# Gated attention and a top-1 expert layer on one core: score columns per query group, mirrors from the last two groups, and a first tile table during attention

## The chip, the cores and the metric

The kernel runs on one core of one Trainium2 chip. Its time is the device time of one execution in microseconds (us). Lower is better.

The engines named here are PE (TensorE: matmuls and transposes, writing to PSUM), ACT (ScalarE), DVE (VectorE), POOL (GpSimd, which here issues DMAs and scatters) and SP (SyncE, which here issues DMAs and DMA transposes).

## The reference

```python
scores = (1.0 / S) * np.matmul(z, z.transpose(0, 2, 1))   # z: 8 x 2816 x 64
attn = np.maximum(scores, 0.0) ** 2
x = (u * np.matmul(attn, v)).reshape(N, D)                # N = 22528, D = 256
y_dense = np.maximum(x @ w1_dense, 0.0) @ w2_dense         # F = 512
logits = x @ w_gate                                        # 8 experts
e = np.argmax(logits, axis=1)                              # one expert per token
gate = softmax(logits)[e]
out = y_dense + gate * (np.maximum(x @ w1[e], 0.0) @ w2[e])
```

The softmax line shortens the original; the rest is its arithmetic. For each batch the score matrix is symmetric: 22 x 22 blocks of 128 x 128.

## The kernel before

**Attention.** A row is 128 queries of a batch, so there are 22 rows per batch and 176 in all (the loop variable g). z is held twice side by side in zT, so that a score matmul contracts over 128 rows, and the scale is halved. `score_chunk` (lines 168 to 176) computes up to four neighbouring blocks of the upper triangle of the scores on PE, applies the relu on ACT into a float32 tile r, and squares r on DVE into the bfloat16 strip A. The blocks below the diagonal are not computed: `mirror` (lines 178 to 190) transposes blocks of A on PE and copies them to a tile T, two copies of three on ACT and one on DVE. `av` (line 223) adds up the 22 matmuls of a row, with A or T as weights and v as the moving operand, and issues the score chunks and mirrors of later rows between them, spread evenly, some seven rows ahead. `gate_x` (line 244) multiplies by u on DVE into `pay`, and SP transposes the row for the logits, which PE computes three rows later. After each 11 rows (a routing group, 16 in all) `route_a` and `route_b` find the expert, the gate and the position of each token, and `scatter` (line 313) writes the rows to the DRAM buffer `xs`, sorted by expert, with one indirect DMA per row on POOL.

**The table.** After the last routing, DVE works out which 256 rows of `xs` and which expert belong to each of 95 tiles (lines 402 to 466). A tile is 256 tokens of one expert.

**Experts.** For each tile SP fetches the tokens transposed (`fetch`, line 475), DVE copies the expert's weights (`expert`, line 487), PE runs `up` and `down` for the dense and for the expert weights, 32 matmuls of 256 columns, and `finish` (line 512) scales, adds and scatters the rows to the output.

**What sets the order.** PE, ACT, DVE and SP run their instructions in the order of the program. Only POOL's order is left to the framework, which may put a DMA there ahead of others. The queues run freely against one another, tied by semaphores. In PSUM the attention has three one-bank buffers for scores, two for transposes, two for the output of `av` and one for the logits; the expert stage opens pools of its own.

Of the kernel before, what the change touches and what calls it, by code (L numbers as in the profile page):

```python
# [15 lines left out]
P = 128  # L16
# [3 lines left out]
def kernel(  # L20
# [18 lines left out]
    assert D == 256 and dq == 64 and F == 512 and E == 8 and S % P == 0  # L39
# [3 lines left out]
    assert nK % G == 0  # L43
    T2 = 256
    NT = N // T2 + E - 1
    ROW = 288
    CAP = N
    XROWS = E * CAP

# [5 lines left out]
    const = ctx.enter_context(tc.tile_pool(name="const", bufs=1))  # L55


    WD = 2 * F + 4 * D
# [6 lines left out]
    ntri = const.tile([P, P], BF, name="ntri")  # L65
    smask = const.tile([P, E, G], F32, name="smask")
# [4 lines left out]
    pays = [const.tile([P, G, ROW], BF, name=f"pay{i}") for i in range(2)]  # L71

    zpool = ctx.enter_context(tc.tile_pool(name="zp", bufs=2))
# [17 lines left out]
    def load_v(b):  # L91
        vb = zpool.tile([P, nK, D], BF, name="vb")
        src = v[b].rearrange("(k p) d -> p k d", p=P)
        for h in range(2):
            k0, k1 = h * nK // 2, (h + 1) * nK // 2
            nc.gpsimd.dma_start(out=vb[:, k0:k1, :], in_=src[:, k0:k1, :])
        return vb

    zT_of, v_of = {}, {}
    make_identity(nc, ident[:])  # L100
    zn0 = load_z(0, parts=4)
    v_of[0] = load_v(0)
# [3 lines left out]
    nc.vector.memset(smask[:, :, 0], 0.0)  # L106
    for p_ in pays:
        nc.vector.memset(p_[:], 0.0)
    nc.vector.memset(ntri[:], -1.0)

# [5 lines left out]
    nc.vector.tensor_copy(desc8[:], ti[:])  # L116
# [3 lines left out]
    nc.vector.tensor_copy(ecap[:], te[:])  # L120
    nc.vector.tensor_copy(base[:], te[:])
    it = const.tile([P, NT], I32, name="it")
    sf = const.tile([P, NT], F32, name="sf")
    itf = const.tile([P, N // T2], F32, name="itf")
    nc.gpsimd.iota(it[:], pattern=[[1, NT]], base=0, channel_multiplier=0)
    nc.vector.tensor_copy(sf[:], it[:])
    nc.vector.tensor_scalar(out=itf[:], in0=sf[:, 0:N // T2], scalar1=float(T2), scalar2=None,
                            op0=ALU.mult)
    pj = const.tile([P, 2], I32, name="pj")
    pjf = const.tile([P, 2], F32, name="pjf")  # L130
    nc.gpsimd.iota(pj[:], pattern=[[P, 2]], base=0, channel_multiplier=1)
    nc.vector.tensor_copy(pjf[:], pj[:])
    one8 = const.tile([P, E], F32, name="one8")
    nc.vector.memset(one8[:], 1.0)

    nc.gpsimd.dma_start(out=wg[:], in_=moe_w_gate.rearrange("(c p) e -> p c e", p=P))


    with tc.tile_pool(name="aA", bufs=1) as aA, \
         tc.tile_pool(name="aT", bufs=2) as aT, \  # L140
         tc.tile_pool(name="aw", bufs=2) as aw, \
         tc.tile_pool(name="rt", bufs=2) as rt, \
         tc.tile_pool(name="psS", bufs=3, space=bass.MemoryType.PSUM) as psS, \
         tc.tile_pool(name="psV", bufs=2, space=bass.MemoryType.PSUM) as psV, \
         tc.tile_pool(name="psT", bufs=2, space=bass.MemoryType.PSUM) as psT, \
         tc.tile_pool(name="psL", bufs=1, space=bass.MemoryType.PSUM) as psL:


        zT_of[0] = zpool.tile([P, nK, P], BF, name="zT")
        for k0 in range(0, nK, 8):  # L150
            k1 = min(k0 + 8, nK)
            nc.vector.tensor_copy(zn0[:, k0:k1, 1, :], zn0[:, k0:k1, 0, :])
            zp = psT.tile([P, 8, P], BF, name="zp", tag="tp")
            for k in range(k0, k1):
                nc.tensor.transpose(out=zp[:, k - k0, :],
                                    in_=zn0[:, k, :, :].rearrange("p h d -> p (h d)"),
                                    identity=ident[:])
            nc.scalar.copy(zT_of[0][:, k0:k1, :], zp[:, :k1 - k0, :])

        A, T, mc = {}, {}, [0]  # L160

        def new_strip(b, k):
            n = nK - k
            A[b, k] = aA.tile([P, n, P], BF, name=f"A{k}", tag=f"A{k}",
                              bufs=2 if k < 4 else 1)

        def score_chunk(b, k, c0, c1):

            zT = zT_of[b]
            w = c1 - c0  # L170
            s_ps = psS.tile([P, 4, P], F32, name="s_ps")
            nc.tensor.matmul(out=s_ps[:, :w, :], lhsT=zT[:, k, :],  # L172
                             rhs=zT[:, k + c0:k + c1, :], start=True, stop=True)
            r = aw.tile([P, 4, P], F32, name="r", bufs=3)
            nc.scalar.activation(r[:, :w, :], s_ps[:, :w, :], AF.Relu, scale=0.5 / S)  # L175
            nc.vector.tensor_mul(A[b, k][:, c0:c1, :], r[:, :w, :], r[:, :w, :])  # L176

        def mirror(b, i, j0, j1):

            if j0 == 0:  # L180
                T[b, i] = aT.tile([P, nK - 1, P], BF, name="T")
            tp = psT.tile([P, 8, P], BF, name="tp", tag="tp")
            for j in range(j0, j1):
                nc.tensor.transpose(out=tp[:, j - j0, :], in_=A[b, i][:, 1 + j, :],  # L184
                                    identity=ident[:])
            mc[0] += 1
            if mc[0] % 3 == 0:
                nc.vector.tensor_copy(T[b, i][:, j0:j1, :], tp[:, :j1 - j0, :])  # L188
            else:
                nc.scalar.copy(T[b, i][:, j0:j1, :], tp[:, :j1 - j0, :])  # L190

        work = []
        total = 0
        strip_end = {}
        for b in range(B):
            for k in range(nK):
                n = nK - k
                nch = -(-n // 4)
                edges = [round(n * j / nch) for j in range(nch + 1)]
                for j in range(nch):  # L200
                    total += edges[j + 1] - edges[j]
                    work.append((total, b, k, edges[j], edges[j + 1], j == 0))
                strip_end[b, k] = total
        wi = [0]

        def chunks(upto):

            jobs = []
            while wi[0] < len(work):
                tot, b, k, c0, c1, first = work[wi[0]]  # L210
                if tot - (c1 - c0) >= upto:
                    break

                def job(b=b, k=k, c0=c0, c1=c1, first=first):
                    if first:
                        new_strip(b, k)
                    score_chunk(b, k, c0, c1)

                jobs.append(job)
                wi[0] += 1  # L220
            return jobs

        def av(b, i, jobs):

            o = psV.tile([P, D], F32, name="o")
            vb = v_of[b]
            done = 0
            for k in range(nK):
                lhsT = A[b, k][:, i - k, :] if k <= i else T[b, i][:, k - i - 1, :]
# [22 lines left out]
        def logits(g):  # L252
            q, j = divmod(g, G)
            if j == 0:
                lg_of[q] = psL.tile([P, G, E], F32, name="lg", tag="lg")
# [322 lines left out]
```

## Time and profile before

| | |
|---|---|
| median of 7 runs | 1053.87 us (1051.4 to 1054.25) |
| the profiled execution, its own time | 1051.9 us |
| its span | 1050.2 us |
| PE busy | 987.2 us (94%) |
| DVE busy | 733.8 us (70%) |
| ACT busy | 655.9 us (62%) |
| POOL busy | 520.9 us (50%) |
| mean clock granted to TensorE | 0.982 of full |

Matmuls are pipelined: the duration of one is longer than the distance to the next, so prices are read from distances. "Busy" of PE counts overlapping matmuls once. A wait line names the waiting engine, its tile and line, what released it, and then the total, the count and the longest. In the view by stage each engine has its busy time and, in brackets, its instructions; the granted clock, the mean busy share of the DMA engines (over 1 where transfers overlap) and GB/s follow. In the timeline the first number is the start, the second how long the merged run of instructions took.

### The profile page before, as it was taken

The numbers are of one execution on the slowest core, as the hardware profiler recorded it, in microseconds if no ns is written. First come the engines' busy times: TensorE is split into PE (matmuls) and PEld (weight loads), VectorE is DVE, ScalarE is ACT, GpSimd is POOL, SyncE is SP. The second block draws the span as 40 slices with busy tenths as digits, with TensorE's granted clock in tenths as the row PEclk, the third lists the DMA queues.
The fourth block names the chain that finished last, engine by engine and source line by source line (L and its number), as shares of the span: only waits on it lengthen the run. The fifth ranks groups of instructions, "written<-read, shape, count | busy, mean of one in ns | idle before, by whom it ended". The sixth has DMA issues, their size and how long they took to land. (4 is left out here: it accounts for less than half of the span.)

```text
span 1050.2 us, 25478 instructions
## 1 busy us (share of the span) xinstructions
PE 987.2 (94%) x9713; PEld 849.2 (81%) x9742; DVE 733.8 (70%) x1638; ACT 655.9 (62%) x994; POOL 520.9 (50%) x528
## 2 busy tenths in 40 slices
PE   5959999999999999999999999909999999999996
PEld 3848888888888888888888888808888888888885
DVE  5838778687787777787777786475666666666664
ACT  6836676776776776676677677205555555555553
POOL 7523452552642642633633524444666666666665
PEclk9989999999999999999999999959999999999999
DMA  8994844745656557367364323314545455555551
GB/s 144 177 166 74 144 107 69 137 104 82 125 97 102 104 103 118 90 111 116 91 114 107 77 68 84 79 36 97 119 110 105 109 120 100 121 107 121 110 113 44
DMA packets 223531, 110.37 MB, mean 105 GB/s; under 512 B 179630, under 2 KB 209070, under 8 KB 223408
## 3 DMA queue, kind: packets, MB, share of 16 engines
q0 software_dynamic: 75264, 79.47, 37.6%
q1 hardware_dynamic: 148144, 29.27, 17.2%
q8 instruction: 76, 1.25, 0.5%
q14 instruction: 47, 0.39, 0.1%
HBM read 61.54 MB, written 39.06 MB: 96 GB/s over the span
## 5 line engine op out<-in xcount | busy, mean ns | idle before, releaser
L176 DVE TENSOR_TENSOR A<-r 128x512 bf16<-128x512 f32 (+2 forms) x576 | 350.6, 624 | 138.9 <-ACT r L175 135.0
L175 ACT ACTIVATE r<-s_ps 128x512 f32<-128x512 f32 (+2 forms) x576 | 308.3, 548 | 129.6 <-PE s_ps L172 90.8
L230 PE MATMUL o<-vb,A 128*128 128x256 bf16 x2024 | 307.8, 273 | 11.3 <-DVE pay L247 10.9
L230 PE MATMUL o<-vb,T 128*128 128x256 bf16 x1848 | 304.0, 273 | 1.2
L501 ACT ACTIVATE h<-h_ps 128x1024 bf16<-128x1024 f32 x190 | 194.4, 1023 | 162.6 <-PE h_ps L498 156.8
L522 POOL DMA_INDIRECT out_dram<-ys,ix x190 | 204.9, 1078 | 137.7 <-DVE ys L520 90.4
L315 POOL DMA_INDIRECT xs<-pay,posi x176 | 196.0, 1114 | 105.4 <-issue 45.7
L230 PEld LDWEIGHTS <-A 128*128 128x128 bf16 x2024 | 180.5, 97 | 45.4 <-issue 11.3
L230 PEld LDWEIGHTS <-T 128*128 128x128 bf16 x1848 | 173.4, 98 | 40.2
L190 ACT COPY T<-tp 128x768 bf16<-128x768 bf16 (+4 forms) x208 | 166.8, 803 | 50.9 <-PE tp L184 47.3
L172 PE MATMUL s_ps<-zT 128*128 128x512 bf16 (+3 forms) x547 | 193.1, 354 | 1.1 <-ACT r L175 1.1
L241 POOL DMA_DIRECT2D ut<-in_u_dram x88 | 65.0, 741 | 226.7 <-DVE pay L247 112.2
L518 DVE TENSOR_SCALAR ys<-ye,me 128x256 f32<-128x256 f32 x190 | 83.2, 480 | 121.0 <-PE ye L508 121.0
L508 PEld LDWEIGHTS <-h 128*128 128x128 bf16 x1520 | 148.7, 98 | 17.9 <-ACT h L501 0.6
L184 PE MATMUL tp<-ident,A 128*128 128x128 bf16 x1848 | 154.5, 219 | 4.5 <-DVE T L188 2.8
L184 PEld LDWEIGHTS <-A 128*128 128x128 bf16 x1848 | 129.0, 98 | 14.6 <-issue 5.5
L498 PE MATMUL h_ps<-xT,w1d 128*128 128x256 bf16 x760 | 99.3, 274 | 22.7 <-DMA xT<-xs 22.7
L498 PEld LDWEIGHTS <-w1d 128*128 128x128 bf16 x760 | 74.6, 98 | 31.8 <-issue 22.9
L498 PE MATMUL h_ps<-xT,we 128*128 128x256 bf16 x760 | 99.3, 274 | 0.0
L508 PE MATMUL ye<-we,h 128*128 128x256 bf16 x760 | 98.5, 273 | 0.3 <-ACT h L501 0.3
L508 PE MATMUL yd<-w2d,h 128*128 128x256 bf16 x760 | 98.5, 273 | 0.0
L247 DVE TENSOR_TENSOR pay<-o,ut 128x256 bf16<-128x256 f32 x176 | 73.5, 418 | 25.2 <-DMA ut<-in_u_dram 15.1
(95 smaller groups left out, 570.3 us busy)
## 6 DMA issues: line engine op xcount, KB each, us to landing
ut<-in_u_dram POOLq DMA_DIRECT2D x88, 256.0 KB
vb<-in_v_dram POOLq DMA_DIRECT2D x16, 704.0 KB
wall<-in_moe_w_dram POOLq DMA_DIRECT2D x16, 256.0 KB
out_dram<-ys,ix POOLq DMA_INDIRECT x190
xT<-pay SPq DMA_TRANSPOSE x176
xs<-pay,posi POOLq DMA_INDIRECT x176
zn<-in_z_dram POOLq DMA_DIRECT2D x7, 352.0 KB
xT<-xs SPq DMA_TRANSPOSE x95
```

What stands on the lines that cost most here:

```text
L172: nc.tensor.matmul(out=s_ps[:, :w, :], lhsT=zT[:, k, :], rhs=zT[:, k + c0:k + c1, :], start=True, stop=True)
L175: nc.scalar.activation(r[:, :w, :], s_ps[:, :w, :], AF.Relu, scale=0.5 / S)
L176: nc.vector.tensor_mul(A[b, k][:, c0:c1, :], r[:, :w, :], r[:, :w, :])
L184: nc.tensor.transpose(out=tp[:, j - j0, :], in_=A[b, i][:, 1 + j, :], identity=ident[:])
L190: nc.scalar.copy(T[b, i][:, j0:j1, :], tp[:, :j1 - j0, :])
L230: nc.tensor.matmul(out=o[:], lhsT=lhsT, rhs=vb[:, k, :], start=(k == 0), stop=(k == nK - 1))
L315: ins = nc.gpsimd.indirect_dma_start(out=xs, out_offset=bass.IndirectOffsetOnAxis(ap=rs[q][:, j:j + 1], axis=0), in_=pays[q % 2][:, j, :]. ...
L498: nc.tensor.matmul(out=h_ps[:, f, :], lhsT=w1(c, f), rhs=xT[:, c, :], start=(c == 0), stop=(c == 1))
L501: nc.scalar.activation(h[:], h_ps[:], AF.Relu)
L508: nc.tensor.matmul(out=y[:, j, :], lhsT=h[:, f, j * P:(j + 1) * P], rhs=w2(f), start=(f == 0), stop=(f == 3))
L518: nc.vector.tensor_scalar(out=ys[:, j, :], in0=ye[:, j, :], scalar1=me[:, j, 0:1], scalar2=None, op0=ALU.mult)
L522: ins = nc.gpsimd.indirect_dma_start(out=out, out_offset=bass.IndirectOffsetOnAxis(ap=ix[:, j:j + 1], axis=0), in_=ys[:, j, :], in_offset= ...
```

## The change

Attention is reorganised by query groups: a batch's 22 rows are cut into groups of 2, 4, 4, 4, 4 and 4. A group has one tile A of 22 key blocks by up to 512 query columns (three such tiles in all). Its blocks are scores for all key blocks, above and below the diagonal, except those that belong to the two groups before it in the batch; these are mirrored from the earlier groups' tiles. A score step takes one or two pairs of key blocks, and a pair fills a two-bank PSUM tile, of which there are three; mirrors, logits and routing share these. The relu takes a pair at once. The square runs on DVE or on ACT, as a small model of the engines' clocks in the program decides while the program is written out; it also decides between which matmuls of `av` the steps go, up to two groups ahead. Mirrors go to DVE or ACT by the same model.

The loads of u go from POOL's queue to SP's. The logits of 11 rows are computed in one burst at their routing. The scatters are spread over more rows, each with a small DVE copy of its index, and a third `pay` tile is added. The expert stage shares the attention's PSUM tiles and the A tiles; `ye` and `yd` share two one-bank buffers, and ACT copies `yd` to SBUF, so that DVE joins scaling and adding in one instruction.

The tile table is made twice. From the first 14 routing groups, a table of 70 full tiles is worked out on DVE between rows 159 and 163, and the first fetches and weight copies are issued at rows 173 to 175. The other 25 tiles come from a second table, made during the expert stage. The two last routings' scatters are not waited for by the first 70 tiles.

The diff, cut to what the prediction speaks of:

```diff
+    Q1 = nQ - 2
+    NT1 = -(-(Q1 * G * P - E * (T2 - 1)) // T2)
+    NT2 = NT - NT1
...
+    NPAIR = 3
+    psS = pool("psS", NPAIR, space=bass.MemoryType.PSUM)
+    psY = pool("psY", 2, space=bass.MemoryType.PSUM)
...
     def load_u(g):
         ut = aw.tile([P, 2, D], F32, name="ut", bufs=3)
-            nc.gpsimd.dma_start(out=ut[:], in_=uf[:, g:g + 2, :])
+        nc.sync.dma_start(out=ut[:], in_=uf[:, g:g + 2, :])
...
+        for w in (2, 4, 4, 4, 4, 4):
+            groups.append((b, i, w))
...
+    clock = {"pe": 0.0, "act": 0.0, "dve": 0.0}
+    def spend(eng, t, after=0.0):
+        clock[eng] = max(clock[eng], after, clock["pe"]) + t
+        return clock[eng]
...
+    def scores(n, k):
...
+        s = psS.tile([P, 2, 4 * P], F32, name="s", tag="s")
+        for h in range(2):
+            nc.tensor.matmul(out=s[:, h, :c], lhsT=zT[:, k + h, :], rhs=zT[:, i0:i0 + w, :],
+                             start=True, stop=True)
+        clock["pe"] += 0.01 + c / 1200
+        r = aw.tile([P, 2, 4 * P], F32, name="r", bufs=3)
+        nc.scalar.activation(r[:, :, :c], s[:, :, :c], AF.Relu, scale=0.5 / S)
+        t = spend("act", 0.09 + c / 600, clock["pe"] + 0.2)
+        freed(t)
+        a = A[n][:, k:k + 2, :c]
+        if max(clock["dve"], t) + 0.07 + c / 480 > clock["act"] + 0.3 + c / 600:
+            nc.scalar.activation(a, r[:, :, :c], AF.Square)
+            t = spend("act", 0.05 + c / 600)
+        else:
+            nc.vector.tensor_mul(a, r[:, :, :c], r[:, :, :c])
+            t = spend("dve", 0.07 + c / 480, t)
...
+    def mirror(n, m, j, nj):
+        (b, i0, w), (_, j0, wj) = groups[n], groups[m]
+        tp = psS.tile([P, nj, w, P], BF, name="tp", tag="s")
...
+    def produce():
+        for n, (b, i0, w) in enumerate(groups):
+            src = [m for m in (n - 2, n - 1) if m >= 0 and groups[m][0] == b]
+            turned = {k for m in src for k in range(groups[m][1], groups[m][1] + groups[m][2])}
+            ks = [k for k in range(0, nK, 2) if k not in turned]
+            seq = [(ks[x:x + 2],) for x in range(0, len(ks), 2)]
+            turns = [(m, 0, groups[m][2]) for m in src]
...
+    def fill(n):
+        while head[0] is not None:
+            m, st, last = head[0]
+            if m > n + 2 or need(st) > clock["pe"] or groups[m][0] not in zT_of \
+                    or clock["act"] > clock["pe"] + 2.0 or clock["dve"] > clock["pe"] + 1.5:
+                return
+            step()
+    def av(n, i):
+        b, i0, w = groups[n]
+        while made[0] < n:
+            step()
...
+        for k in range(nK):
+            nc.tensor.matmul(out=o[:], lhsT=A[n][:, k, (i - i0) * P:(i - i0 + 1) * P],
+                             rhs=v_of[b][:, k, :], start=(k == 0), stop=(k == nK - 1))
+            clock["pe"] += 0.11
+            if k % 2 == 1:
+                fill(n)
...
+    def scatter(g):
+        q, j = divmod(g, G)
+        pi = rt.tile([P, 1], I32, name="pi", bufs=6)
+        nc.vector.tensor_copy(pi[:], rs[q][:, j:j + 1])
...
+        if q < Q1:
+            nodep(ins, ["xs"], "xs")
+        else:
+            nodep(ins, ["xs", "xs2"], "xs", "fx")
...
+            nc.vector.scalar_tensor_tensor(out=ys[:, j, :], in0=ye[:, j, :], scalar=me[:, j, 0:1],
+                                           in1=yd[:, j, :], op0=ALU.mult, op1=ALU.add)
...
+            ydp = down(hd, lambda f: w2d[:, f, :], "yd")
+            yd = take("yd")
+            nc.scalar.copy(yd, ydp[:])
...
+    at(4, zero_fill)
...
+    t1 = Q1 * G + 5
+    for n, fn in enumerate(table(0, NT1)):
+        at(t1 + n // 2, fn)
+    for s in range(AHEAD):
+        at(nB - AHEAD + s, lambda s=s: got.update({s: fetch(s)}))
+    for s in range(2):
+        at(nB - 2 + s, lambda s=s: wes.update({s: expert(s)}))
+    t2 = nB + 45
+    for n, fn in enumerate(table(1, NT2)):
+        at(t2 + n, fn)
```

`at(row, f)` runs f after that row's `av` and `gate_x`; numbers from 176 on are tiles of the expert stage. `step` issues the next score step or mirror of the stream that `produce` lists; `need` gives the modelled time at which as many PSUM pairs are free as the step takes, and `freed` records when one will be.

## The prediction

> **What bounds the kernel now.** I read the busy times first: PE 987.2 us of a span of 1050.2 us, DVE 733.8, ACT 655.9. So the question is which parts of the span PE does not fill. The view of busy time by stage, cut where PE starts or stops (engines in the order of its head line, then the granted clock of TensorE), answers it:
>
> ```profile
> core 0: us, PE busy (x) PEld busy (x) DVE busy (x) ACT busy (x) POOL busy (x), PEclk, DMA share, GB/s
> 20.60:64.70 44.10, 41.87 (x434) 34.72 (x433) 30.50 (x56) 34.02 (x59) 24.24 (x34) 1.00 1.24 178
> 64.70:74.00 9.30, 0.16 (x4) 0.09 (x3) 0.51 (x2) 0.52 (x1) 0.00 (x0) 0.77 1.31 163
> ...
> 80.00:680.10 600.10, 595.78 (x6130) 506.11 (x6157) 456.29 (x1025) 412.32 (x721) 261.50 (x262) 1.00 0.53 100
> 680.10:708.10 28.00, 1.00 (x12) 0.53 (x11) 19.66 (x48) 0.28 (x1) 13.61 (x12) 0.57 0.14 41
> 708.10:714.00 5.90, 5.89 (x40) 4.63 (x41) 0.16 (x1) 2.62 (x3) 0.00 (x0) 0.71 0.34 56
> 714.00:1040.00 326.00, 326.00 (x2989) 292.20 (x2987) 208.24 (x466) 190.72 (x187) 200.97 (x186) 1.00 0.52 110
> ```
>
> PE is full in attention (595.8 of 600.1 us) and in the expert stage (326.0 of 326.0). It is empty in two holes: 64.7 to 74.0, and 680.1 to 708.1 between the stages. The waits (total, times, longest) say why; the last line is from SP's own queue:
>
> ```profile
> PE h_ps L498 <- DMA xT<-xs: 22.7, 1, 22.7
> ...
> DVE pay L247 <- DMA ut<-in_u_dram: 15.1, 2, 11.2
> ...
> PE o L230 <- DVE pay L247: 10.9, 2, 9.1
> ...
> SPq L476 <- DVE Rt L450: 18.1, 1, 18.1
> ```
>
> The first hole is a late tile of u: gate_x waits 11.2 us, and PE behind it 9.1. The second is the chain last logits, routing, tile table, first fetch: SP waits 18.1 us for the table's Rt, PE 22.7 us for the fetch. The timeline gives unit prices, as the distance from one start to the next:
>
> ```profile
> 301.20 0.61 PE L184 MATMUL tp<-ident,A 128*128 128x128 bf16 x8
> 301.65 0.60 PE L230 MATMUL o<-vb,T 128*128 128x256 bf16 x4
> 302.08 0.38 PE L172 MATMUL s_ps<-zT 128*128 128x512 bf16 x1
> 302.30 0.71 PE L230 MATMUL o<-vb,T 128*128 128x256 bf16 x5
> ...
> 13.15 6.24 ACT L175 ACTIVATE r<-s_ps 128x512 f32<-128x512 f32 x12
> ...
> 300.09 1.89 DVE L176 TENSOR_TENSOR A<-r 128x512 bf16<-128x512 f32 x3
> 301.89 0.42 DVE L247 TENSOR_TENSOR pay<-o,ut 128x256 bf16<-128x256 f32 x1
> 302.23 0.55 DVE L176 TENSOR_TENSOR A<-r 128x384 bf16<-128x384 f32 x1
> 302.69 0.68 DVE L188 COPY T<-tp 128x1024 bf16<-128x1024 bf16 x1
> 303.30 0.68 DVE L176 TENSOR_TENSOR A<-r 128x512 bf16<-128x512 f32 x1
> ```
>
> Eight transposes take 0.45 us (0.056 each), an AV matmul 0.11, a 512-column score 0.22. On ACT a 512-column relu follows the last by (6.24-0.60)/11 = 0.51; on DVE a square by (1.89-0.69)/2 = 0.60, a gate takes 0.34, a 1024-column mirror copy 0.61.
>
> **Part 1, scores and mirrors.** PE's work per batch before: 484 AV x 0.11 = 53.2; 231 mirrors x 0.056 = 12.9; 41 scores of 512 columns, 28 of 384, 3 smaller = 13.8; 22 logits pairs x 0.05 = 1.1. That is 81.0 us, 648 for eight batches. Check: 20.6 to 680.1 is 659.5; less the hole of 9.3 and about 1.3 at the lower clock after it leaves 648.9. So PE was essentially unstalled elsewhere. After: the widths 2,4,4,4,4,4 with at most two earlier groups mirrored give 44+80+64+3x56 = 356 scored blocks (253 before) and 8+24+3x32 = 128 mirrored ones (231). 78 scores of 512 columns and 22 of 256 are 19.6 us, 128 mirrors 7.2, AV 53.2, logits in bursts of 22: 22 x 0.028 x 2 = 1.2 (the four in a row at 680.11 start 0.028 apart). Sum 81.2. **PE: 0**; the ends are -3 (what rounding of the unit prices can hide) and +10 if each of the 352 weight loads of the logits shows its 0.055.
>
> What does change is ACT and DVE. A pair is now 1024 columns: by the rows, relu 0.51+0.43 = 0.94 on ACT, square 0.60+0.53 = 1.13 on DVE. Per batch 39 full pairs and 11 half ones: relu 42.3, squares 50.7. Mirror copies (nine of up to 2048 columns at 0.53 ns) 9.2, gates 22 x 0.34 = 7.5, two routings of 4.2 (sum of the sixteen small DVE rows of lines 267 to 310) 8.4, the new one-column copy ahead of each scatter 22 x 0.15 (between the rows 0.117 and 0.185) 3.3. Together 121 us for two engines in 2 x 81 = 162: 75%. All squares on DVE would be 79, at the bound; the planner sends a square to ACT when DVE is still busy as the relu ends, so about every other one. That puts ACT near 65 and DVE near 55. It fits, but group by group it is uneven: group 1 with 10 pairs takes 10 x 0.94 + 5 x 0.9 = 13.9 of ACT against 14.6 us of PE, and group 0 is over. Working up to two groups ahead smooths that. PE takes its work in order, so every score that waits for one of the three PSUM pairs holds the AV matmuls behind it. No row shows the new waits. Bounds: -4 (the 4.3 us now idle between 80 and 680 vanish) and, from above, 27 score steps and 7 mirrors per batch, 272 in all, each late by 0.14 us (an unoverlapped 0.08 of one relu, 0.60 minus 0.51, plus 0.06 of hop): +38. The rows of back-to-back work do overlap, which is nearer the low end; but exp waited 32.8 us in all for DVE's d, 16 times, and ACT's relus queue behind it with PE now closer behind. So I go a quarter of the way up: **+6.**
>
> A page speaks against this part. The Trainium skill, "ScalarE: Activation LUTs", Rules for kernel authors, wants relu and products on VectorE, since it is up to about 3 times faster in bf16; here L176 reads float32, and 0.60 us against 0.51 for 512 columns says ACT is no slower. The same page, Table sets, names relu, copy and identity as filler of every set but not Square; if exp and Square lay in different sets, 16 exps would cost 32 loads, by the page's 2.66 us 85 us of ACT.
>
> The trace has one table load, 1.28 us, for relu, copy and exp. If Square needed its own, two more for each of the 16 exps would be 41 us of ACT, 5 per batch of 81 us, inside ACT's slack of 16; I take 0 and leave the rest to the upper end.
>
> **Part 2, u on SP's queue.** 88 issues of 0.74 us (65.0 us) leave POOL. The late tile was issued at 57.59, after sixteen weight loads since 28.5, and used at 73.49. POOL's order is not written by hand, so the weights will still run ahead and the DMA share of 1.24 to 1.31 remain; but u no longer stands behind them in one queue. It stands behind SP's transposes instead: zT(1) took 11.15 us at 57.78, xT some 1.2, and load_u leads its use by four rows, 4 x 3.7 = 14.8 us. Ends: -10.6 (9.3 and 1.3 of clock) and 0 (the same wait by another queue). **-8.** The load is on SP ahead of the next xT; what waits for xT is only the logits at the end of a routing group, three rows on.
>
> The Trainium skill, "DMA: Bandwidth & Descriptors", Issuing engines are not separate DMA queues, says that all issuers share 16 DMA engines, so a change of issuer saves only issue time; by it this term would be about 0, while the queue order in the row above is why I don't follow it.
>
> **Part 3, the first table during attention.** The chain of 680.1 to 708.1 leaves the path: table and routing of the first 14 routing groups are ready rows before, fetches are issued at rows 173 to 175, weights copied at 174 and 175. 70 of 95 tiles come from it, so the last two routings and the second table have 70 x 3.49 us of cover. -28.0, and -1.7 for the first tile's half clock (two bursts of eight matmuls at 1.87 us against 1.04); some 0.7 stays at the seam. **-29**; ends -29.7 and -24, if expert(0) or fetch(0) still waits for POOL's last weights (0.8 each) and scatters (1.1 each). Moved with it: three fetches (1.21 and 0.42 on SP each) among the last xT on SP, where nothing else is due, and up to 22 scatters that POOL now issues between the expert stage's own: one in two tiles, 2.16 + 0.55 of 3.49 us. DVE pays for it in attention: two rows of 0.89 on 704 columns, seven of 0.72 (0.95 on 760 scaled to 560) and small ones, about 8 us in five rows (18.5 us) where it already works 55/81: 20.5 of 18.5. **+2**, ends 0 and +4.
>
> **Part 4, start.** AV began at 20.6 behind twelve chunks. Now 11 half pairs must be done: relu and squares 5.6+6.6 shared by two engines, 6 us and a hop after zT, and DVE no longer waits 3.3 us for POOL's iota before copying z. But v's 2.9 MB must land too (the first 20 us moved 3.0 MB), and group 1 costs ACT and DVE 12 us while PE has 9.7. The 16 zero fills of 0.55 on POOL become 8, z and v come in 3 and 4 parts: hidden behind v's transfer, 2 us if not. **+2**, ends -3 and +6.
>
> **Part 5, expert stage.** PE's 32 matmuls of 0.109 are 3.49 us per tile. ACT gains one 128x512 copy (0.60, as a relu) on two relus of 1.02: 2.64 of 3.49. DVE loses the 0.69 addition and the 0.15 index. yd and ye now share two buffers; yd is read 0.2 after its end or after relu(he), by 1 us into the next tile, and reused only 2.5 us later. **0**; ends 0 and +5.
>
> Sum: 0+6-8-29+2+2+0 = -27. The profiled execution took 1051.9 us (span 1050.2 and 1.7 around it); the median of the seven runs is 1053.87, 2 above. So 1024.9 by the one and 1026.9 by the other; I say 1026.
>
> **Rivals.** A: attention becomes bound by ACT and DVE in part. For: 75% load on both, in-order PE, exp blocking ACT. Against: PE idled only 4.3 us in 600 with 412 and 456 us of ACT and DVE. At +25 to +40 in place of +6: 1045 to 1060.
> B, slower: the PSUM handover, and it alone. Place: the 272 steps waiting for relu or copy. The other terms gain 33, so it decides from 33/272 = 0.12 us per step; at 0.25 (two unoverlapped relus at 0.08, and 0.09) it costs 68 us: 1053.9-33+68 = 1089. Against: ACT ran twelve relus back to back at 0.51 through three buffers.
> C: holes and bubbles all vanish: 1053.9-29.7-10.6-4-3 = 1007.
> D: the table does not leave the path, because fetch(0) waits for all scatters after all. Then part 3 is worth some -8 (the table's DVE work without the routing) and the time is 1026+21 = 1047. Against: rows 168 (last scatter that it needs) and 173 are 18 us apart.
>
> **How the numbers follow.** My forecast, 1012 to 1040: 0.60. C, below 1012: 0.10. D, faster: 0.05. A: 0.13, of it 0.07 faster, 0.03 within, 0.03 slower. B: 0.12, slower. What a measurement can tell from no change is about 0.2%, 2 us. Faster 0.82, same 0.03, slower 0.15. The range, 1006 to 1052, leaves out B, the upper half of A and the edge of C: 0.20.
>
> **What would show it.** Right: PE busy across the change of stage with no wait of h_ps for xT over 2 us; no wait of DVE for ut over 2 us near 65; transposes 1024, score matmuls 800; ACT above 65/81 busy in attention. Wrong: PE waits "s from ACT r" or "tp from DVE A" over 30 us in total; more than one table load; PE below 95% in the middle of attention; a tile period above 3.6 us.

## The result, and the profile after

The changed kernel takes 1057.16 us (median of 15 runs, 1054.79 to 1060.18), the kernel before 1053.55 us (37 runs beside them). The ratio is 1.0037, 95% interval 1.0029 to 1.0046: slightly slower, where 1026 us was predicted, and outside the range that was given. The profiled execution took 1059.02 us, its span is 1057.3 us.

Where the 7.1 us between the two profiled spans come from can be read off the gates of the rows (`gate_x`, line 247 before and 334 after), of which there are 176, evenly through attention:

| stretch (us) | before | after | difference |
|---|---|---|---|
| start to the gate of row 21 (batch 0) | 117.65 | 114.55 | -3.1 |
| batches 1 to 6 (81.34 each before, 85.80 after) | 488.05 | 514.82 | +26.8 |
| batch 7 | 74.61 | 77.39 | +2.8 |
| last gate to the first expert matmul | 27.80 | 1.17 | -26.6 |
| first to last expert matmul | 334.13 | 337.69 | +3.6 |
| from there to the end of the span | 7.96 | 11.68 | +3.7 |

So the hole between the stages went, as forecast, and attention gave the same amount back in small pieces. The view of busy time by stage, for one whole batch, the seam, and the expert stage:

```profile
core 0: us, PE busy (x) PEld busy (x) DVE busy (x) ACT busy (x) POOL busy (x), PEclk, DMA share, GB/s
224.19:310.00 85.81, 81.79 (x752) 65.27 (x761) 56.06 (x113) 63.65 (x74) 26.53 (x25) 1.00 0.52 100
706.76:718.00 11.24, 7.53 (x51) 5.72 (x52) 3.25 (x8) 3.62 (x5) 2.98 (x3) 0.85 0.35 75
728.00:1040.00 312.00, 312.00 (x2861) 279.02 (x2859) 142.82 (x339) 225.00 (x268) 195.91 (x192) 1.00 0.49 114
```

In the batch PE idles 4.0 of 85.81 us. DVE is busy 56 and ACT 64 of 86, near the shares that the prediction worked out, and neither is full. The expert stage is as full as before. PE's waits (total, times, longest):

```profile
PE o L322 <- DVE pi L408: 14.9, 15, 1.5
PE zp L144 <- DVE zn L141: 7.5, 1, 7.5
PE s L228 <- ACT r L232: 5.1, 12, 0.8
PE s L228 <- DVE A L260: 4.1, 9, 0.5
PE h_ps L585 <- DMA xT<-xs: 3.5, 2, 2.3
```

The largest is not one of the waits that the prediction looked for. It is `o`, the sum of a row, and it waits for DVE. L408 is the small copy of an index that stands right behind a row's gate; the gate is what frees the buffer of `o`, and there are two such buffers. The timeline shows how the gate comes to be late (the 22 products that start at 220.08 are those of row 48, those at 224.17 belong to row 49; the gate at 223.70 is row 47's):

```profile
218.61 1.92 ACT L232 ACTIVATE r<-s 128x1024 f32<-128x1024 f32 x2
...
219.65 1.23 DVE L240 TENSOR_TENSOR A<-r 128x1024 bf16<-128x1024 f32 x1 [0.56 <-ACT r L232]
...
220.08 2.57 PE L322 MATMUL o<-vb,A 128*128 128x256 bf16 x22
220.56 1.06 ACT L237 ACTIVATE A<-r 128x1024 bf16<-128x1024 f32 x1
221.52 1.01 ACT L232 ACTIVATE r<-s 128x1024 f32<-128x1024 f32 x1
222.56 1.23 DVE L240 TENSOR_TENSOR A<-r 128x1024 bf16<-128x1024 f32 x1 [1.69 <-ACT r L232]
223.70 0.42 DVE L334 TENSOR_TENSOR pay<-o,ut 128x256 bf16<-128x256 f32 x1
224.04 0.14 DVE L408 CAST pi<-pos 128x1 int32<-128x1 f32 x1
...
224.17 0.60 PE L322 MATMUL o<-vb,A 128*128 128x256 bf16 x4 [1.52 <-DVE pi L408]
```

Row 47's sum is complete when row 48's products start. DVE stands idle for 1.69 us and still doesn't do the gate, because a square is ahead of it in program order, and that square waits for a relu which ACT reaches only after two relus and a square of its own. The gate runs 3.6 us late, and PE stands at row 49 for 1.52 us. ACT's round of relu, relu, square takes 2.9 us (starts 215.69, 218.61 and 221.52); the program's model has 2.79 for it, and lets steps be issued while ACT is up to 2.0 us ahead of PE's clock.

At the seam, PE's and then SP's own rows:

```profile
707.93 1.05 PE L585 MATMUL h_ps<-xT,w1d 128*128 128x256 bf16 x8 [1.21 <-DMA xT<-xs]
...
713.44 1.33 PE L585 MATMUL h_ps<-xT,w1d 128*128 128x256 bf16 x8 [2.30 <-DMA xT<-xs]
714.57 1.92 PE L595 MATMUL ye<-ring 128*128 128x256 bf16 x8
```
```profile
704.97 1.20 SPq L539 DMA_TRANSPOSE xT<-xs  x1
...
706.91 1.20 SPq L336 DMA_TRANSPOSE xT<-pay  x1
708.92 1.41 SPq L539 DMA_TRANSPOSE xT<-xs  x1
...
711.07 1.67 SPq L336 DMA_TRANSPOSE xT<-pay  x1
713.23 1.22 SPq L539 DMA_TRANSPOSE xT<-xs  x1
```

PE goes over to the experts almost at once, but the second tile is late: SP issues its three fetches (L539) in turn with the transposes of the last rows, some 4 us apart, each behind its row's gate, and the second was issued at 708.92, when PE was already at the first tile. PE waits 2.30 us for it, and the granted clock from 713.4 to 717.7 is 0.60: the eight matmuls at 714.57 take 1.92 us where 1.04 is usual.

The last line of the table is SP's wait at the end of the program, first of the changed kernel and then of the one before:

```profile
SPq L730 <- PEq L730: 6.7, 2, 6.1
```
```profile
SPq L573 <- PEq L573: 1.9, 2, 1.4
```

### The profile page after: what moved, and what is told of

It reads as the page before. It is cut to its first block, busy times and chain, and to the rows that moved or that the text cites. A ratio compares the mean times of both kernels' runs of the same rounds, so it can differ in the third digit from the quotient of the medians.

```text
span 1057.3 us, 23813 instructions
## 1 busy us (share of the span) xinstructions
PE 997.0 (94%) x9070; PEld 824.0 (78%) x9142; DVE 610.5 (58%) x1276; ACT 752.5 (71%) x880; POOL 426.7 (40%) x433
## 4 chain that ended last, share of the span: by engine, by line
PE 47%; ACT 19%; issue 15%; DVE 12%; POOL 5%; DMA 1%; POOLq 0%; another core or an unknown queue 0%; ACTq 0%; DVEq 0%; SPq 0%
PE o L322 21%; ACT r L232 16%; PE h_ps L585 9%; DVE A L240 6%; POOL out_dram L612 5%; PE ye L595 5%; PE yd L595 5%; PE s L228 4%; PE tp L250 3%; ACT A L237 2%; DVE A L260 2%; DVE pay L334 2%; DMA zn<-in_z_dram 1%; PE lg L344 0%; DMA xT<-xs 0%
## 5 line engine op out<-in xcount | busy, mean ns | idle before, releaser
L322 PE MATMUL o<-vb,A 128*128 128x256 bf16 x3872 | 478.7, 273 | 19.0 <-DVE pi L408 14.9
L232 ACT ACTIVATE r<-s 128x1024 f32<-128x1024 f32 (+1 forms) x400 | 348.6, 920 | 116.6 <-PE o L322 87.7
L240 DVE TENSOR_TENSOR A<-r 128x1024 bf16<-128x1024 f32 (+1 forms) x225 | 243.0, 1089 | 204.5 <-ACT r L232 203.7
L409 POOL DMA_INDIRECT xs<-pay,pi x176 | 180.7, 1027 | 411.2 <-DVE pi L408 306.5
L588 ACT ACTIVATE ring<-h_ps 128x1024 bf16<-128x1024 f32 x190 | 194.5, 1024 | 116.0 <-PE h_ps L585 110.8
L228 PE MATMUL s<-zT 128*128 128x512 bf16 (+1 forms) x728 | 190.9, 358 | 14.5 <-ACT r L232 5.1
L612 POOL DMA_INDIRECT out_dram<-ring,me x140 | 143.5, 1025 | 88.0 <-DVE ring L609 60.1
L237 ACT ACTIVATE A<-r 128x1024 bf16<-128x1024 f32 (+1 forms) x175 | 171.7, 981 | 5.7
L595 PEld LDWEIGHTS <-ring 128*128 128x128 bf16 x1520 | 148.7, 98 | 19.0 <-ACT ring L588 1.1
L595 PE MATMUL ye<-ring 128*128 128x256 bf16 x760 | 99.4, 274 | 0.3 <-ACT ring L588 0.3
L585 PEld LDWEIGHTS <-ring 128*128 128x128 bf16 x760 | 74.6, 98 | 9.1
L260 DVE COPY A<-tp 128x2048 bf16<-128x2048 bf16 (+1 forms) x72 | 79.1, 1099 | 2.6 <-PE tp L250 2.6
```

What stands on the lines that cost most here:

```text
L228: nc.tensor.matmul(out=s[:, h, :c], lhsT=zT[:, k + h, :], rhs=zT[:, i0:i0 + w, :], start=True, stop=True)
L232: nc.scalar.activation(r[:, :, :c], s[:, :, :c], AF.Relu, scale=0.5 / S)
L237: nc.scalar.activation(a, r[:, :, :c], AF.Square)
L240: nc.vector.tensor_mul(a, r[:, :, :c], r[:, :, :c])
L260: nc.vector.tensor_copy(dst, src)
L322: nc.tensor.matmul(out=o[:], lhsT=A[n][:, k, (i - i0) * P:(i - i0 + 1) * P], rhs=v_of[b][:, k, :], start=(k == 0), stop=(k == nK - 1))
```

## The experiments

**Theory.** The 4.46 us per batch are waits for gates that stand behind squares on DVE, whose relus ACT delivers late because the planner packs ACT too tightly. **Rivals:** PE's own work has grown; the three score pairs bind; the table's work on DVE or u's place on SP's queue cost more than they gain. The batches in the middle of attention repeat to 0.1 us for the same code in the changed kernel and in the one with the smaller lead, on every chip of these runs, so their attention is compared across runs by its gates. (Single batches of other variants, and the kernel before with u moved, do differ between chips by up to some 2 us.) Whole times are compared within one chip only: most runs were on chips where the kernel before itself took 1149 to 1175 us (more on this at the end).

**1. Squares left out.**

```diff
-        nc.scalar.activation(r[:, :, :c], s[:, :, :c], AF.Relu, scale=0.5 / S)
+        nc.scalar.activation(a, s[:, :, :c], AF.Relu, scale=0.5 / S)
...
-            nc.scalar.activation(a, r[:, :, :c], AF.Square)
...
-            nc.vector.tensor_mul(a, r[:, :, :c], r[:, :, :c])
```

> The squares are left out: the relu writes straight into A, so the output is the one of a plain relu and 172 us of ACT and 243 us of DVE are gone, while PE's order of work stays the same to the instruction. Theory (PE's 4.8 us of waits per batch come from work that ACT and DVE deliver late): the batch period falls from 85.8 us to about 81.3, the waits of PE for DVE and ACT in attention to under 0.5 us per batch, and the time from 1057 to about 1020. Rival (PE's own stream is slower: fewer transposes but other weight loads, bursts of logits): the period stays above 84.5 us and the time above 1050.

Batches 3 to 6 took 80.50 to 80.69 us, and PE's waits between 187 and 660 us are 1.3 us in all. The first two after the start-up batch took longer, 85.16 and 82.45 us; in the first of them PE waits 1.5 us for the routing on DVE and 1.1 us for ACT, and its granted clock is 0.98. The rest of what they lose is not explained. The view of one batch:

```profile
350.71:431.22 80.51, 80.04 (x753) 65.54 (x761) 27.86 (x84) 43.30 (x52) 25.06 (x25) 1.00 0.58 107
```

PE does its whole batch in 80.5 us. So the 85.8 of the changed kernel are not PE's work, and its waits come from what ACT and DVE do. The whole time was 1066.96 us, 0.910 of the 1174.91 us of the kernel before on that chip.

**2. A smaller lead.**

```diff
-                    or clock["act"] > clock["pe"] + 2.0 or clock["dve"] > clock["pe"] + 1.5:
+                    or clock["act"] > clock["pe"] + 0.8 or clock["dve"] > clock["pe"] + 1.5:
```

> One number is changed: the planner issues no further step while ACT's modelled clock is over 0.8 us ahead of PE's (2.0 before). Theory (gate_x stands on DVE behind a square that waits for ACT's queue, and PE's next row but one waits for the output buffer that gate_x frees): the wait of av for DVE falls from 14.9 us to under 4 us, the period to 82 to 83.5 us, the time to 1030 to 1045. Rival (ACT and DVE lack throughput, the lead is needed): waits move to A not being ready, the period stays at 85.8 or grows, the time is 1055 or more.

> The changed kernel with one number other: its planner lets ScalarE run at most 0.8 us ahead of TensorE where it had 2.0, as in the second experiment, whose batches took 81.25 us where the changed kernel's take 85.80. Theory (the squares that the planner packs too closely make the row's gate late, and the next row but one waits for its buffer): the last attention row's gate at 677, not 706.8, everything behind it as in the changed kernel, so 1057 - 30 = 1027 us, against 1053.9 before. Rival (the wait is only moved, and the seam or the expert stage gives it back): 1040 or more.

The same squares on the same engines, only issued later against PE. Batches 1 to 5 took 81.25 us in all four runs of this kernel, the last gate came at 677.03 to 677.40 us (706.76 in the changed kernel, 680.31 before). One batch of a later run of it, and PE's waits of that run from 113 to 677 us, all of them:

```profile
275.97:357.23 81.26, 81.10 (x762) 65.51 (x761) 55.78 (x114) 63.98 (x75) 24.59 (x25) 1.00 0.60 106
```
```profile
PE pre L376 <- DVE oh L363: 1.2, 1, 1.2
PE s L228 <- DVE d L355: 0.9, 1, 0.9
PE s L228 <- ACT r L232: 0.4, 1, 0.4
```

DVE 55.8 and ACT 64.0 us of work are what they were with 85.8; the waits of `o` are gone. So it is the position of the work, not its amount. The 29.4 us by which the last gate comes earlier are the effect of this one number in the planner. On its first two chips the kernel took 1078.75 and 1079.88 us (kernel before: 1174.91 and 1173.92; ratios 0.918 and 0.920), not the 1027 of the expectation, since the stage of the experts was disturbed there (389.7 and 386.0 us from first to last matmul, 337.7 in the result). Two more were made for its time alone:

> The changed kernel with the planner's limit for ScalarE at 0.8 us ahead of TensorE (it had 2.0), to be timed on a chip where the kernel before takes 1053: the two runs of it so far were on chips where that took 1174. Theory: last attention row's gate near 677 instead of 707, seam, expert stage and end as in the changed kernel, 1056 - 30 = 1026 us. Rival: 1040 or more.

> The changed kernel with a lead of 0.8 us for ScalarE, once more for its time, since the chips of its three runs slowed the stage of the experts. Theory: 1056 - 30 = 1026 us where the kernel before takes 1053. On a chip where that takes 1150 to 1175, 1077 to 1080 as before, and the time stays open there.

Both fell on one other disturbed chip: 1076.53 us against 1149.39 (0.936), and 1071.34 against 1158.32 (0.924). The time of this kernel on a chip like that of the result stays unmeasured. From its gates it would be 1056 less 29.4, some 1027 us; that is an estimate.

**3. No step late in a row.** The lead stays at 2.0.

```diff
-            if k % 2 == 1:
+            if k % 2 == 1 and k < 14:
                 fill(n)
```

> The changed kernel with its lead of 2.0 us, but no score or mirror step is issued behind the last eight of a row's 22 products, so that the squares of these steps don't stand ahead of the row's gate on VectorE. Theory (the gate stands in line behind late squares): the wait of o for the gate (15 waits in the changed kernel's page, 14.9 us, and more that its records leave out) falls to below a third, and a batch takes 81 to 83.5 us, where the changed kernel's take 85.80. Rival (the two engines are behind as a whole, wherever their steps stand): 85 us or more, as the steps only crowd into the first part of the row.

This run and the two of experiment 4 were on a chip like that of the result. PE's waits from 111 to 692 us, and before them those of the changed kernel from 114.55 to 706.7:

```profile
PE o L322 <- DVE pi L408: 14.4, 14, 1.5
PE s L228 <- DVE A L260: 3.3, 7, 0.5
PE lg L344 <- DVE A L260: 3.1, 7, 0.4
PE s L228 <- ACT r L232: 2.4, 8, 0.3
```
```profile
PE o L322 <- DVE pi L408: 8.0, 14, 0.8
PE s L228 <- ACT r L232: 4.4, 15, 0.3
PE s L228 <- DVE A L260: 2.9, 6, 0.5
```

A batch took 84.13 us, between the two expectations: the gate's wait nearly halved and did not fall to a third, and `s` waits 2.0 us longer for ACT. So the squares of a row's last eight products are a part of the cause. What is left is of the same kind. Here are DVE's and then PE's rows around the gates of rows 95 and 96 (400.54 and 400.93):

```profile
399.40 1.23 DVE L240 TENSOR_TENSOR A<-r 128x1024 bf16<-128x1024 f32 x1 [1.69 <-ACT r L232]
400.54 0.42 DVE L334 TENSOR_TENSOR pay<-o,ut 128x256 bf16<-128x256 f32 x1
400.87 0.14 DVE L408 CAST pi<-pos 128x1 int32<-128x1 f32 x1
400.93 0.41 DVE L334 TENSOR_TENSOR pay<-o,ut 128x256 bf16<-128x256 f32 x1
```
```profile
401.01 0.38 PE L322 MATMUL o<-vb,A 128*128 128x256 bf16 x2 [0.77 <-DVE pi L408]
```

A square issued earlier in the row keeps DVE waiting 1.69 us for its relu, two gates stand behind it, and PE waits 0.77 us. Moving the steps forward in the row takes away some of the squares ahead of the gate, but not ACT's delay of those that remain. The last gate was 15.05 us earlier than in the changed kernel on the same chip (692.36 against 707.41), and the median 12.3 us less: 1043.71 us, 0.991 of the kernel before (0.989 to 0.993). What is gained in attention does come through to the end. This version is faster than both kernels.

**4. Both kernels again, on that chip.**

> The kernel before, unchanged, for its trace on a chip of the experiments, where it took 1174 us (1053.9 where it was first measured). Theory: its instructions last as long as before, and engines stand still in stretches that the profile puts down to issue and to nothing, in attention around the loads of v and the weights (batch period 90 to 96 us where it was 81.34, as the kernel with u moved had 95) and in the expert stage. Rival: attention as before at 81.34, all 120 us in the expert stage.

> The changed kernel, unchanged, on the same chip as the run before it. Theory: its attention stage is as in its first profile (batch period 85.8, last row's gate at 706 to 708), the expert stage 35 to 55 us longer, as in the third and fourth experiment: 1100 to 1112 us, ratio to the kernel before 0.94 to 0.95, so that the order of the two kernels is another than in the result. Rival: 1120 or more, with an attention stage that is longer too.

1053.35 and 1055.99 us, ratio 1.003 (1.0019 to 1.0041): the result repeats, and neither expectation held, as they reckoned with a disturbed chip. The batches took 81.34 and 85.75 us, the gap at the seam 27.75 and 1.27 us, the end from the last expert matmul 7.94 and 11.71 us. Only two lines of the table moved: the start (121.20 and 115.54 us to the gate of row 21), and the stage of the experts, 334.66 and 335.41 us, where PE waited 0.61 us for the second tile's fetch and 0.92 for the third's.

**5. Four buffers for o, two pairs.**

```diff
-    NPAIR = 3
+    NPAIR = 2
...
-    psY = pool("psY", 2, space=bass.MemoryType.PSUM)
+    psY = pool("psY", 4, space=bass.MemoryType.PSUM)
```

> The changed kernel with the eight banks of PSUM dealt otherwise: two pairs for scores and mirrors where there were three, and four buffers for the sums of an attention row (o) where there were two; the planner's limit of 2.0 us stays. Theory (TensorE stands at the next row but one because only two o buffers are there): the wait of o for the gate goes, and a batch takes 81 to 84 us instead of 85.80, unless two pairs are too few, which shows as waits of s for ScalarE. Rival (what was thought when the change was costed: the pairs are what binds): a batch takes 88 us or more, with the waits on s. The expert stage has fewer buffers for h too and is not compared.

Batches 2 to 6 took 88.3 to 89.3 us. PE's largest waits from 112 to 724 us:

```profile
PE o L322 <- DVE A L260: 10.3, 7, 1.7
PE s L228 <- ACT A L263: 9.9, 6, 1.7
PE s L228 <- DVE A L260: 9.7, 15, 1.3
```

The wait for the gate is gone, as the theory said of it, but the number is the rival's: with two pairs the waits are on the pairs, and `o` waits for a mirror copy (L260) that writes what it reads, not for its buffer. With a whole bank for each `o`, as here, the eight banks don't hold three pairs and more than two `o`. So this run agrees with the theory that the gate's wait needs the two `o` buffers, but doesn't show it alone, as PE was also slower in it; nor does it show that more buffers would have been worth having. The time was 1132.00 us (0.964 of 1173.92 on that chip).

**6. u back on POOL's queue, in the changed kernel.**

```diff
-        nc.sync.dma_start(out=ut[:], in_=uf[:, g:g + 2, :])
+        nc.gpsimd.dma_start(out=ut[:], in_=uf[:, g:g + 2, :])
```

> The loads of u go back to POOL's queue, all else as in the changed kernel. Theory (u's late tile came from its place behind the weight loads in POOL's queue): DVE waits again for u by 8 to 12 us around row 8, PE stands 6 to 10 us there, and the time is 1063 to 1069. Rival (all issuers share the DMA engines, so the queue does not matter; or the attention's new rhythm hides it): no wait for u over 2 us and the time within 2 us of 1057.

No wait for u came back: the gate of row 21 was at 113.33 us (114.55 with SP), batches took 85.86 (the sixth 86.68). From 30 to 100 us POOL stands at the load of u until a gate frees its buffer, and DVE nowhere waits for `ut`:

```profile
POOL ut L119 <- DVE pay L334: 17.9, 4, 7.3
```

In the changed kernel's attention the queue of u is worth nothing. The time of this run, 1112.27 us (0.946 of before), was on the first disturbed chip.

**7. u on SP's queue, in the kernel before.** The same line the other way round, twice:

> The kernel before, with the 88 loads of u alone moved from GpSimd's queue to SP's, where they stood in the changed kernel. In the kernel before, TensorE had a hole of about 10 us from 64.7 to 74.0, behind u. Theory as predicted (the queue makes it): the hole goes, 1053.9 - 8 to - 10 = 1044 to 1046, from the gate of row 21 on. Rival (after the third experiment: the order of what stands ahead of u on the queue makes it, and another part of the change removes the hole, or SP's own transposes now make u late): within 3 us of 1053.9.

> The kernel before with u alone moved from GpSimd's queue to SP's, where the kernel before takes 1053 (on the other chip its attention was disturbed all over). Theory of the prediction: TensorE's hole of 10 to 11 us behind u in batch 0 goes, 1043 to 1046. Rival: within 3 us of 1053, so the hole in the changed kernel went by something else.

Both were on disturbed chips (1188.93 and 1168.73 us, 1.011 and 1.014 of before there), so their times can't be read, only the start of attention. The gates of rows 0 to 5 are the same to 0.04 us as in the first trace; the 10.9 us in which PE waited for gates that waited for u are gone, and this stands in their place:

```profile
PE lg L258 <- DMA xT<-pay: 5.9, 1, 5.9
```

The gate of row 16 is at 97.03 and 96.75 us, 101.10 before: 4.1 to 4.4 us gained. How firm that is, the second trace of the kernel before shows (experiment 4): it has the same hole, its gate of row 16 at 104.65, and is the same as the first trace until row 5. Against it the gain is 7.6 to 7.9 us. At the gate of row 21 (119.03 and 117.16 us, 117.65 and 121.20 in the kernel before) little or nothing is left of it; one idle stretch of PE lies between, 3.4 and 2.7 us, that the profile puts down to "issue". The DMA engines are just as busy between 50 and 75 us (share 1.29 and 1.30, 1.31 before), and what is late next is a row's transpose. So the queue was a cause of the wait for u, worth 4 to 8 us at row 16, and what of it reaches the end isn't shown; in the changed kernel the hole is gone with either queue, so something else took it away there. There, row 8 (the row that waited) has its gate at 70.1 us where it had wanted it near 62, so the loads have 8 us more; that this is the reason was not tried.

**8. The first table behind the last row.** Its count stays where it was; the rest, the first fetches and copies come after attention.

```diff
-        at(t1 + n // 2, fn)
+        at(t1 if n == 0 else nB + 4 + n // 2, fn)
...
-        at(nB - AHEAD + s, lambda s=s: got.update({s: fetch(s)}))
+        at(nB + 13 + s, lambda s=s: got.update({s: fetch(s)}))
```

> The first table (all but the count of tokens) and the first fetches and weight copies go behind the last routing again, so the chain of routing, table and fetch lies between the two stages as before the change. Theory (the seam is worth what it cost): PE is empty for 24 to 30 us between the last av and the first expert matmul, the time is 1080 to 1086. Rival (the early table costs the attention about as much as it saves: DVE delays PE in the last batch): 1060 to 1070.

> The changed kernel with its first table and fetches behind the last row: 1056 + 18 to + 24 = 1074 to 1080 us where the kernel before takes 1053; the seam's gap 18 us as on two other chips. Rival: less than 1070, the table's 2 us on VectorE in attention being more than that.

The seam, in PE's rows of the last of three runs (the other two: gaps of 18.15 and 18.05 us, and the same waits):

```profile
711.15 0.20 PE L344 MATMUL lg<-wg,xT 128*128 128x8 bf16 x2 [2.19 <-DMA xT<-pay]
...
726.03 1.86 PE L585 MATMUL h_ps<-xT,w1d 128*128 128x256 bf16 x8 [12.58 <-DMA xT<-xs]
```

From the last gate (707.89) to the first expert matmul are 18.1 us, where the changed kernel has 1.2 to 1.3, and the first bursts run at half the clock (granted clock 0.50 from 725 to 729 us, 1.86 us for eight matmuls). The 24 to 30 us of the first expectation were too many. So the place of the last routing, the table and the fetches is worth some 17 us, and the clock up to 1.7 more. The other 9.7 of the 26.6 can be read off the two seams. The table takes DVE 12.5 us in the kernel before (687.49 to 699.99) and 7.0 here (715.41 to 722.37), with 70 tiles for 95, fewer columns to work out and the count already made. From there to the first expert matmul are 8.1 us before and 3.7 here. In the kernel before, SP waits for scatters in between, as its queue from 680 to 712 us shows:

```profile
SPq L481 <- DMA xs<-pay,posi: 4.3, 3, 1.6
```

The changed kernel doesn't wait for the last two routings' scatters. The table's work on DVE lies in batch 7, which is 0.9 us shorter without it (76.46 against 77.36); batch 6 is the same (85.75 and 85.74). The times, 1112.21, 1107.04 and 1104.41 us (0.950, 0.962 and 0.954 of before), are from disturbed chips, where the changed kernel itself was not timed; neither forecast of the whole time can be settled by them.

**9. Fetches three rows earlier, with the smaller lead.**

```diff
-        at(nB - AHEAD + s, lambda s=s: got.update({s: fetch(s)}))
+        at(nB - 6 + s, lambda s=s: got.update({s: fetch(s)}))
```

> As the run before it, and the fetches of the first three expert tiles issued at rows 170, 171 and 172 instead of 173, 174 and 175. Theory (the second tile waits 2.3 us because SP's queue works off transposes of attention rows and fetches one after the other): that wait and the half clock behind it go, 2 to 4 us under the run before it, so 1023 to 1025. Rival (the fetches hold up the last rows' own transposes, or the rows of the first tiles are not there yet and SP stands at them): the wait stays or grows, 1027 or more.

> That and the first three fetches at rows 170 to 172, on the same chip. Theory: the 2.3 to 3.5 us that TensorE waits for the first tiles' transposes go, 1022 to 1024. Rival: same as the run before it within 1 us, the wait is taken over by another.

PE's rows at the seam of the second run:

```profile
677.11 1.04 PE L585 MATMUL h_ps<-xT,w1d 128*128 128x256 bf16 x8
...
680.14 1.04 PE L585 MATMUL h_ps<-xT,w1d 128*128 128x256 bf16 x8
```

No expert matmul waits for a fetch any more, and the first starts before the last gate. Against the smaller lead alone on the same chip it is 4.0 us less (1075.87 against 1079.88) and 6.4 less (1070.09 against 1076.53); a third pair, where 2 to 4 were expected, gave 0.4 (1070.96 against 1071.34). The waits are gone in all three; what that is worth in time was not settled to better than these.

## Why the prediction was wrong

| term (us) | predicted | measured | by |
|---|---|---|---|
| PE's own work | 0 | -0.6 | with the smaller lead: five batches of 81.25 (81.34 before), the last 0.2 shorter |
| bubbles in attention | +6 | +29.4 | last gate, changed kernel less smaller lead |
| u's queue and the start | -8 + 2 | -4.1 | gate of row 21 with the smaller lead (113.53), against 117.65 |
| first table on DVE | +2 | +0.9 | batch 7, changed kernel against experiment 8 |
| a stop in batch 6 | none | +1.8 | batch 6 with the smaller lead, 83.1 against 81.25 |
| the seam | -29 | -26.6 | last gate to first expert matmul |
| the expert stage | 0 | +3.6 | first to last expert matmul (+0.75 in experiment 4) |
| the end | none | +3.7 | SP's wait at the end |

The table's 0.9 us lie in batch 7 and are contained in the other rows; without it, those add up to 7.2, the difference of the two spans to 0.1. The stop in batch 6 stands between the gates of rows 145 and 146 (8.2 us apart, 6.4 in the other batches), where DVE begins a routing 1.9 us late, some 50 us ahead of the first table. It is in all four runs with the smaller lead; what DVE waits for there is open.

**The step that failed is the bubble term of part 1.** Its bounds, -4 and +38, held the measured 29.4; the value in them was chosen a quarter of the way up, where about four fifths would have been right, and that is 23 of the 31 us by which the forecast missed. (The upper bound counts seven mirror steps per batch where the copies a few lines above it are nine, and its 0.06 us of hop stands in no row; with nine it is +40, which changes little.) The choice leaned on rows of back-to-back work that overlapped well, and on engine totals of 75%. Both were true: ACT and DVE did come to 64 and 56 of 86 us. Totals say nothing about a queue. The place was wrong too: the prediction put the late handover on the three score pairs and asked for waits of s or tp above 30 us. They came to 5.1 for s behind ACT, 4.1 for s behind a mirror copy and 0.3 for tp, and the main wait was `o` behind the gate, on a buffer that the change had left at two. What was not asked is what stands ahead of the gate in DVE's order, and how long it may wait there: in the kernel before, one relu per square, and in the changed one two relus and a square of ACT's. The runs showed that in its place: with the planner's lead for ACT cut from 2.0 to 0.8 us, the gate's wait is gone and the 29.4 us with it, at the same work on both engines (experiment 2).

**Rival A, attention bound in part by ACT and DVE**, given 0.13, came nearest: +25 to +40 in place of +6, and 1045 to 1060 us. Its size and time held. Its words didn't quite: experiment 2 ran the same work on both engines without the wait. Of the signals named, PE's share in the middle of attention stopped at 95.3%, just short of the 95% that was to show the prediction wrong, and the count of table loads and the tile period of 3.49 us were as forecast.

**Part 2** was worth at most what it was given, and in the changed kernel nothing, for a reason that the prediction names and then sets aside. The Trainium skill, "DMA: Bandwidth & Descriptors", section "Issuing engines are not separate DMA queues", says that all issuers share the 16 DMA engines. Experiment 6 agrees with it (0 in the changed kernel). Experiment 7 agrees in part: a transpose became late by 5.9 us in u's place, but the gate of row 16 came 4 to 8 us earlier, though that of row 21 did not. The 3 to 4 us that the start gained in the changed kernel are thus not u's queue; what they are was not tried.

**Part 3** was right in mechanism and to 2.4 us in size, and its cost on DVE, 0.9 us, lies within its ends. It missed that something is due among those fetches on SP: they stand behind the last rows' transposes, and PE pays 3.5 us for it (1.2 for the first tile, 2.3 for the second) and the low clock behind that. Experiment 9 takes these waits away. **Part 1's aside** on the table sets held: the Trainium skill, "ScalarE: Activation LUTs", section "Table sets", doesn't count Square among the fillers, but the trace after has one table load of 1.28 us, with relu, copy, exp and 175 squares on ACT. **The end** had no term at all. It is 3.7 us on either chip where both kernels ran; SP waits 6.1 to 6.6 us for PE's queue in the changed kernel and its variants (6.6 with u on POOL), 5.9 in the kernel before with u on SP, and 1.4 in the kernel before. What causes it was not tried and stays open.

## What to carry to other kernels

When work is moved onto an engine that runs in program order, ask of every short instruction on it that frees a buffer (here a 0.4 us gate) what stands ahead of it, what that waits for, and how many buffers the producer has left; totals of busy time don't answer this. If a hand-written planner decides the order, compare its costs and its allowed lead with the trace's cadence first, because one number of it was worth more here than the rest of the change. When the bounds of a bubble term are wide and no row shows the queue, the friendly end is not the safe choice; here it was 23 us off.

## What the runs showed of the hardware

The same program can be some 10% slower on another chip. The kernel before took 1053.35 us on the chip of experiments 3 and 4, and 1174.91, 1173.92 and 1149.39 to 1158.32 us on three others. Single instructions last as long there (an expert matmul 273 to 275 ns, a relu of the experts 1.02 us). What differs is idle time, part of it put down to "issue" or to nothing. In the kernel before with u moved, a batch took 93 to 97 us, and the batch view has PE and the granted clock down together:

```profile
212.64:306.93 94.29, 86.53 (x837) 70.68 (x836) 63.09 (x142) 56.67 (x101) 28.19 (x26) 0.95 0.48 91
```

The changed kernel, with u on either queue and its table early or late, has nearly the same attention on all chips (most batches 85.75 to 85.87 us, single ones up to 87.4; 81.25 with the smaller lead), and its variants lose in the experts' stage: 363.6 to 391.2 us from first to last matmul, 335.1 to 337.7 on undisturbed chips. So on those chips every variant of the changed kernel that computes the whole is 4 to 8% faster than the kernel before, the ones with the table behind the last row too, while on the chip of the result the two are within 0.4%. What the chips differ in, or whether it is the chip at all and not the hour, is open.
